# Loading a matrix of 113 rows in two transfers, 112 rows and one

## The chip, the cores and the metric

The kernel runs on one core of a Trainium2 chip. The core has five engines with an instruction queue each: TensorE (PE, matmuls, with a row of its own for weight loads, PEld), VectorE (DVE), ScalarE (ACT), GpSimd (POOL) and SyncE (SP, which only issues transfers here). Sixteen DMA engines move the data between the device memory and the core; SyncE, GpSimd and ScalarE give them their work. The metric is the time of one execution on the device in microseconds, the median of several.

## The reference, cut to what matters

A block of two parts with a residual each: a state-space convolution (S4) over 2048 positions and 576 channels with 128 complex states per channel, and a gated MLP that mixes positions. Both are modulated by six vectors made from a condition vector `c`.

```python
x = A_u
mod = (_silu(c) @ w_mod).reshape(c.shape[0], 6, 1, -1)
sa, ca, ga, sb, cb, gb = (mod[:, i] for i in range(6))
h = _layernorm(x) * (1 + ca) + sa
x = x + ga * ssm(h, A_re, A_im, B_re, B_im, C_re, C_im, log_dt, Dskip)
h = _layernorm(x) * (1 + cb) + sb
x = x + gb * mlp(h, w_in, w_sp, b_sp, w_out)

# ssm: K[d, l] = Re sum_n C[d, n] * exp(dt[d] * A[d, n] * l) * dt[d] * B[d, n], dt = exp(log_dt)
#      y = the causal convolution of h with K (by FFTs of length 4096) + h * Dskip
```

## The kernel before, in words

The function `ssm` makes the convolution, the class `Mlp` the rest. The change lies in the first lines of `ssm` that issue work.

**What the start makes.** Three strands run beside each other in the first 90 us. The *poles*: for each state, the logarithm of its decay, its phase and so on are computed on VectorE and ScalarE from seven inputs (`poles`), split into three bfloat16 parts, written to the device memory (`pa_d`, `pb_d`) and read back in another layout as the tiles `lb`, `lc` and `la` (`poles_load`). `p0` is this for the first 144 channels (tile `et` as staging), `p1` for the other 432 in one go (tiles `t_n_...`, steps `q`). The *modulation*: for each k, `mod_load` brings a part of `w_mod` (two transfers of 96 rows; tile `wm` or `k`), `mod_mm` multiplies it with silu(c), `mod_ev` copies the partial sums out (`mpart`), `mod_on` sums them over the partitions by a matmul with a matrix of ones, and `mod_fin` stores the row (`gar`, `cga`, `sga`). The matrix of ones is the last of six 128x128 matrices in the tile `small`. The *norm of the input*: `ln_load` brings x (tile `ln_x`), `ln_stat` makes mean and variance, `ln_row` and `ln_mm` go on with it.

**The selection matrix.** `sel` is a tile of 113 partitions and 2368 bfloat16 columns, read from `c_sel`. Matmuls with `lb`, `lc` or `la` as weights and columns of `sel` as the moving operand (`e_mm`, `ec_mm`, `phase`, `t_unit`) spread the poles over times. They read rows 0 to 47 and 64 to 111, or 0 to 111; those of `phase` with x = 0 read rows 0 to 48 and 64 to 112. Row 112 holds constants for these alone.

**What sets the order.** In the opening every engine runs its instructions in the order of the program (`tied`, class `Pinned`); SyncE, too. SyncE's transfers are, in this order: seven of the poles, `cT` (c), two of `wm` (k = 2), `sel`, two of `k` (k = 1), `small`, two of `lb`, two each of `lc` and `la`, seven of `t_n_...`, `dsk`. GpSimd's are the writes of the poles, `ln_x`, `k` (k = 0), `r1t`, `cs`, `msk` and the second `ln_x`. After that the string `OPENING` names one step after the other; it begins with

```python
"mo 2;mm 1;ml 3;mg 2;me 1;eA 0;w 0 0;mo 1;EA 0;w 0 1;eB 0;..."
"EA 2;mm 0;EB 2;mf 1;q 0;r 0;a 0;me 0;q 1;mo 0;mf 0;q 2;c 0;..."
```

where `mo` is `mod_on`, `mm` is `mod_mm`, `eA` is `e_mm`, `a` and `c` are `phase`, and `q 0` starts `p1` with the activation `t_dt`. From about 207 us to about 445 us a loop over ticks makes the rest of the convolution, and there the order on an engine is planned by the program's scheduler; behind it stretches are written out again.

Of the kernel before, what the change touches and what calls it, by code (L numbers as in the profile page):

```python
# [121 lines left out]
def body(tc, I, out):  # L122
    nc = tc.nc
    V, A, G, T, S = nc.vector, nc.scalar, nc.gpsimd, nc.tensor, nc.sync
    with ExitStack() as ctx:
        dram = ctx.enter_context(tc.tile_pool(name="dram", bufs=1, space=DRAM))
        keep = ctx.enter_context(tc.tile_pool(name="keep", bufs=1))

        x1_d = dram.tile([16, 128, D], F32, name="x1_d")

        consts_s = keep.tile([128, 4], F32, name="consts_s")
        V.memset(consts_s[:, 0:1], MAGIC)
        V.memset(consts_s[:, 1:2], math.pi / 2)
        V.memset(consts_s[:, 2:3], 1.0)
        V.memset(consts_s[:, 3:4], 0.0)
        mod_d = dram.tile([3, D], F32, name="mod_d")
        acc = keep.tile([128, 96], F32, name="acc")
        m = Mlp(tc, ctx, I, x1_d, dram, mod_d, acc, out)
        ssm(tc, I, x1_d, consts_s, dram, mod_d, m)
        m.phase_a()  # L140
        m.phase_b()
# [47 lines left out]
def ssm(tc, I, x1_d, consts_s, dram, mod_d, mlp):  # L189
    nc = tc.nc  # L190
    V, A, G, T, S = nc.vector, nc.scalar, nc.gpsimd, nc.tensor, nc.sync
# [3 lines left out]
    with ExitStack() as ctx:  # L195
# [22 lines left out]
        sel = tb.tile([113, 2368], BF, name="sel", bufs=1)  # L218
# [109 lines left out]
        def poles_tile(c, Q):  # L328
            for n, p in (("lb", 112), ("lc", 113), ("la", 113)):
                lt[n, c] = tb.tile([p, 9, 128], BF, name=n)  # L330
                Q.memset(lt[n, c][32:64], 0.0 if n == "lb" else 1.0)
                if n != "lb":
                    Q.memset(lt[n, c][96:113], 1.0)
# [35 lines left out]
        def mod_load(k, Q):  # L369

            if k < 2:
                t = kp.tile([128, 32, 128], F32, name="k1").rearrange("p a b -> p (a b)")
                wmt[k] = [t[:96, 6 * HC * hh:6 * HC * hh + 6 * HC].rearrange("p (k n) -> p k n", k=6) for hh in range(2)]
            else:
                wmt[k] = [ep.tile([96, 6, HC], F32, name="wm") for hh in range(2)]
            for hh in range(2):
                Q.dma_start(wmt[k][hh], I["w_mod"][:, k, hh])
# [434 lines left out]
        V, A, G, T, S = mlp.tied.vector, mlp.tied.scalar, mlp.tied.gpsimd, mlp.tied.tensor, mlp.tied.sync  # L812
        p0 = poles(0, 1, G, tb.tile([128, 1536], F32, name="et", bufs=5))
        S.dma_start(cT, I["c"])
        mod_load(2, S)
        S.dma_start(sel, I["c_sel"])
        mod_load(1, S)
        S.dma_start(small, I["c_small"][:, 128:].rearrange("p (i c) -> p i c", i=6))
        poles_tile(0, G)
        for _ in range(4):  # L820
            next(p0)
# [38 lines left out]
        V, A, G, T, S = nc.vector, nc.scalar, nc.gpsimd, nc.tensor, nc.sync  # L860
# [40 lines left out]
        V, A, G, T, S = mlp.nc.vector, mlp.nc.scalar, mlp.nc.gpsimd, mlp.nc.tensor, mlp.nc.sync  # L901
# [1427 lines left out]
```

## Time and profile before

| | us |
|---|---|
| median of 3 runs | 1800.42 (1796.09 to 1802.07) |
| the profiled execution | 1799.91 |
| its span | 1798.0 |
| TensorE busy | 1673.5 (93%) |
| VectorE busy | 1244.5 (69%) |
| ScalarE busy | 819.0 (46%) |

The span runs from the first to the last instruction of the profiled execution; the time of that execution has 1.9 us more around it. Engines work beside each other, so their busy times don't add up to the span. The timeline gives start, duration, engine, line, operation, and in brackets how long the engine was idle before it and what released it; nearly every line reads L154, because a helper records the pinned instructions there, so tiles tell them apart. For a transfer the timeline shows its issue on the queue's engine, and the DMA issues give the time to its landing.

### The profile page before, as it was taken

The numbers are of one execution on the slowest core, as the hardware profiler recorded it, in microseconds if no ns is written. First come the engines' busy times: TensorE is split into PE (matmuls) and PEld (weight loads), VectorE is DVE, ScalarE is ACT, GpSimd is POOL, SyncE is SP. The second block draws the span as 40 slices with busy tenths as digits, with TensorE's granted clock in tenths as the row PEclk, the third lists the DMA queues.
The fourth block names the chain that finished last, engine by engine and source line by source line (L and its number), as shares of the span: only waits on it lengthen the run. The fifth ranks groups of instructions, "written<-read, shape, count | busy, mean of one in ns | idle before, by whom it ended". The sixth has DMA issues, their size and how long they took to land.

```text
span 1798.0 us, 36706 instructions
## 1 busy us (share of the span) xinstructions
PE 1673.5 (93%) x15374; PEld 1247.2 (69%) x15374; DVE 1244.5 (69%) x2242; ACT 819.0 (46%) x1095; POOL 252.6 (14%) x397
## 2 busy tenths in 40 slices
PE   0498899998799989999999999999999999999999
PEld 0154555565455544777877888887888888888887
DVE  4576589975898998788899677689344468344432
ACT  1477799864377666444534343334222124122110
POOL 2023234233122212000000000000111100111100
PEclk7669999999899999999999999999999999999999
DMA  7355946579778778777674887773666573556531
GB/s 206 82 159 172 262 128 176 167 200 291 233 230 279 253 235 268 255 264 254 241 234 140 282 289 264 240 264 124 229 237 221 202 234 107 188 201 207 202 110 41
DMA packets 181468, 376.28 MB, mean 209 GB/s; under 512 B 38325, under 2 KB 101429, under 8 KB 180534
## 3 DMA queue, kind: packets, MB, share of 16 engines
q1 hardware_dynamic: 137766, 171.43, 31.6%
q0 software_dynamic: 37632, 175.83, 29.6%
q10 hardware_dynamic: 5904, 26.67, 3.6%
q8 instruction: 121, 1.98, 0.5%
q14 instruction: 45, 0.37, 0.1%
HBM read 263.12 MB, written 101.31 MB: 203 GB/s over the span
## 4 chain that ended last, share of the span: by engine, by line
PE 42%; DVE 18%; issue 9%; DMA 7%; ACT 3%; POOL 1%; ACTq 0%; SPq 0%; DVEq 0%; POOLq 0%
PE ps L154 40%; DMA zset<-set_d 4%; DVE zset L154 4%; DVE gt L154 2%; DVE bsz L154 2%; DMA raw<-z_d 1%; ACT z L154 1%; DVE n L154 1%; DVE rq L154 1%; DVE wsp L154 1%; DVE raw L154 1%; DVE wout L154 1%; DVE wso L154 1%; DVE z L154 1%; DMA uu<-v_d 1%
## 5 line engine op out<-in xcount | busy, mean ns | idle before, releaser
L154 PEld LDWEIGHTS <-zset 128*128 128x128 f16 x7182 | 702.7, 98 | 95.5 <-DVE zset L154 7.5
L154 PE MATMUL ps<-wsp,zset 128*128 128x256 f16 x6048 | 669.4, 273 | 9.0 <-DVE zset L154 5.8
L154 PE MATMUL pz<-wz,nt 128*128 128x512 f16 (+1 forms) x1120 | 222.3, 358 | 11.2 <-DVE nt L154 4.3
L154 ACT ACTIVATE z<-gt 128x1024 f16<-128x1024 f32 x56 | 59.0, 1054 | 292.6 <-DVE gt L154 292.6
L154 PEld LDWEIGHTS <-nt 128*128 128x128 f16 x1120 | 108.9, 98 | 118.3 <-DVE nt L154 5.8
L2037 POOL DMA_DIRECT2D zset<-set_d x96 | 50.8, 530 | 872.4 <-PE ps L154 632.1
L154 DVE SCALAR_TENSOR_TENSOR gt<-ps,sc,bsp 128x512 f32<-128x512 f32 x36 | 27.0, 750 | 207.2 <-PE ps L154 205.5
L154 PE MATMUL ps<-wout,z 128*128 128x288 f16 x1344 | 170.0, 286 | 0.0
L154 PEld LDWEIGHTS <-z 128*128 128x128 f16 x1344 | 131.5, 98 | 33.0
L154 DVE TENSOR_TENSOR raw<-raw 128x512 f32<-128x512 f32 (+2 forms) x228 | 119.2, 528 | 14.7 <-DMA raw<-z_d 10.4
L154 PE MATMUL ps<-n2o,zset 128*128 128x256 f16 x1134 | 128.2, 273 | 0.0
L154 DVE SCALAR_TENSOR_TENSOR gt<-ps,sc,gt 128x512 f32<-128x512 f32 (+1 forms) x180 | 122.2, 696 | 7.6
L154 ACT ACTIVATE zset<-raw 128x1792 f16<-128x1792 f32 x48 | 81.0, 1690 | 55.3 <-PE ps L154 18.7
L154 DVE TENSOR_TENSOR zset<-raw,zset 128x1792 f16<-128x1792 f32 x48 | 96.9, 2019 | 13.1 <-ACT zset L154 13.1
L154 DVE TENSOR_TENSOR z<-ps,z 128x512 f32<-128x512 f32 (+1 forms) x126 | 72.0, 599 | 37.2 <-ACT z L154 26.7
L154 ACT ACTIVATE wsp<-raw,sc 128x1792 f16<-128x1792 f32 x25 | 44.6, 1785 | 43.1 <-DVE raw L154 35.4
L154 ACT ACTIVATE z<-z,sc 128x1024 f32<-128x1024 f32 x21 | 24.1, 1148 | 76.0 <-DVE z L154 72.3
L154 ACT ACTIVATE z<-pz,sc 128x512 f32<-128x512 f32 (+1 forms) x96 | 51.6, 583 | 12.7 <-PE pz L154 6.1
L154 ACT ACTIVATE z<-z,nm,r 128x1152 f32<-128x1152 f32 x24 | 31.5, 1342 | 56.7 <-DVE nm L154 31.4
L154 PE MATMUL ps<-n2q,wf 128*128 128x512 f16 x252 | 55.7, 379 | 0.0
L154 PE MATMUL ps<-wout,z1b 128*128 128x288 f16 x384 | 52.4, 286 | 0.0
L154 DVE SCALAR_TENSOR_TENSOR wsp<-raw,sc,wsp 128x1792 f16<-128x1792 f32 x25 | 52.0, 2078 | 0.0
(353 smaller groups left out, 2441.7 us busy)
## 6 DMA issues: line engine op xcount, KB each, us to landing
zset<-set_d POOLq DMA_DIRECT2D x96, 896.0 KB, 4.9
raw<-z_d SPq DMA_DIRECT2D x48, 512.0 KB, 5.6
set_d<-zset ACTq DMA_DIRECT2D x24, 896.0 KB, 6.6
z_d<-z POOLq DMA_DIRECT2D x32, 576.0 KB, 9.2
zset<-wa_d POOLq DMA_DIRECT2D x18, 896.0 KB, 4.9
raw<-in_w_spT SPq DMA_DIRECT2D x25, 512.0 KB, 5.0
set_d<-zset SPq DMA_DIRECT2D x12, 896.0 KB, 4.6
u_d<-st1o POOLq DMA_DIRECT2D x16, 576.0 KB, 4.1
```

The costliest lines, as they stand in the source:

```text
L154: return self.tc.keep_in_program_order(f(*a, **k))
L2037: self.nc.gpsimd.dma_start(o, self.set_d[f, j - 1] if j else self.wa_d[f])
```

## The change

The load of `sel` is split. The first 112 rows go where the whole load was, the last row goes behind `small`. Nothing else differs: the same bytes go to the same tile on the same queue.

```diff
         S.dma_start(cT, I["c"])
         mod_load(2, S)
-        S.dma_start(sel, I["c_sel"])
+        S.dma_start(sel[:112], I["c_sel"][:112])
         mod_load(1, S)
         S.dma_start(small, I["c_small"][:, 128:].rearrange("p (i c) -> p i c", i=6))
+        S.dma_start(sel[112:], I["c_sel"][112:])
         poles_tile(0, G)
```

## The prediction

> **What bounds the kernel now.** I read the page's head and its 40 slices first, then the waits of TensorE over the first 70 us, because a load issued in the first microseconds can only matter there. Columns of the waits: waiting engine and tile, what ended the wait, us in total, times, longest.
>
> ```profile
> span 1798.0 us, 36706 instructions
> PE   0498899998799989999999999999999999999999
> ...
> PE ps L154 <- DMA small<-in_c_small: 39.4, 1, 39.4
> ```
>
> The span is 1798.0 us and the execution took 1799.9 us. In the first slice of 45 us TensorE is hardly busy; later it is busy nearly always. One wait of 39.4 us, for the small matrices, makes that hole. The timeline (start, us, engine, line, operation) shows what is in the queue around it:
>
> ```profile
> 5.44 0.33 SPq L154 DMA_DIRECT2D sel<-in_c_sel  x1
> 5.82 12.12 SPq L154 DMA_DIRECT2D k<-in_w_mod  x2
> 17.27 0.75 POOL L154 DMA_DIRECT2D pb_d<-pt  x1
> 17.98 3.40 SPq L154 DMA_DIRECT2D small<-in_c_small  x1
> 22.32 0.78 POOL L154 DMA_DIRECT2D pa_d<-pt  x1 [3.74 <-DVE pt L154]
> 25.79 4.34 SPq L154 DMA_DIRECT2D lb<-pb_d  x2
> 50.08 2.25 SPq L154 DMA_DIRECT2D la<-pa_d  x2
> 53.58 0.42 SPq L154 DMA_DIRECT2D t_n_log_dt<-in_A_log_dt  x1
> 54.43 0.38 SPq L154 DMA_DIRECT2D t_n_A_im<-in_A_A_im  x1
> 54.55 2.26 PE L154 MATMUL ps<-mpart,small 128*128 128x288 f32 x4 [39.40 <-DMA small<-in_c_small]
> 56.74 3.32 PE L154 MATMUL ps<-k,ec 96*32 96x288 f32 x24
> 59.99 0.39 PE L154 MATMUL ps<-sel,lb 48*128 48x512 bf16 x2
> 66.42 0.58 ACT L154 ACTIVATE t_dt<-t_n_log_dt 128x432 f32<-128x432 f32 x1
> 71.68 0.60 DVE L154 TENSOR_TENSOR t_q<-t_n_C_im,t_n_B_im 128x432 f32<-128x432 f32 x1
> ```
>
> The sel load takes 0.33 us to issue, and right behind it two loads hold SyncE for 12.12 us. What the transfers move meanwhile is in the windows (stretch, length, busy times and counts of PE, PEld, DVE, ACT, POOL, granted clock, DMA share, GB/s):
>
> ```profile
> 6.00:8.00 2.00, 0.00 (x0) 0.00 (x0) 1.91 (x8) 0.00 (x1) 0.11 (x1) 1.00 0.88 276
> 8.00:10.00 2.00, 0.00 (x0) 0.00 (x0) 1.92 (x7) 0.61 (x1) 0.00 (x0) 1.00 0.97 252
> 10.00:12.00 2.00, 0.70 (x8) 0.39 (x10) 1.83 (x8) 1.95 (x5) 0.00 (x0) 1.00 0.36 96
> 12.00:14.00 2.00, 2.00 (x18) 0.75 (x12) 0.47 (x3) 1.83 (x5) 0.00 (x0) 1.00 0.06 26
> 44.00:46.00 2.00, 0.00 (x0) 0.00 (x0) 0.00 (x0) 0.00 (x0) 0.00 (x0) 0.50 0.07 28
> ```
>
> From 12 to 14 us, and again from 44 to 46, the share is 0.06 to 0.07 of 16 DMA engines: one engine works, at 26 to 28 GB/s, and fifteen stand still. Which transfer it is, the DMA issues (KB each, median us to landing), the tile view of the k loads (ns of one, shortest, median, longest; first and last start) and SyncE's own waits say:
>
> ```profile
> sel<-in_c_sel SPq DMA_DIRECT2D x1, 522.6 KB
> k<-in_w_mod SPq DMA_DIRECT2D x2, 648.0 KB, 37.6
> small<-in_c_small SPq DMA_DIRECT2D x1, 384.0 KB, 36.4
> pa_d<-pt POOLq DMA_DIRECT2D x3, 108.0 KB, 8.0
> t_n_log_dt<-in_A_log_dt SPq DMA_DIRECT2D x1, 216.0 KB, 6.2
> ...
> L154 SPq DMA_DIRECT2D k<-in_w_mod x2: 1999/6040/10081, 5.8 to 15.9; - x2
> ...
> SPq L154 <- DMA sel<-in_c_sel: 14.1, 1, 14.1
> SPq L154 <- DMA pb_d<-pt: 4.3, 1, 4.3
> ```
>
> 522.6 KB are 0.535 MB; at 26 GB/s one engine needs 20.6 us for them, and longer while the transfers of POOL's queue share that engine from 15 to 44 us. SyncE waited 14.1 us for sel before la, so sel landed just before 50.08, 44.6 us after its issue. The second k load (issued at 15.9, 37.6 to its landing) landed at 53.5 and small at 17.98 + 36.4 = 54.4: both hold a small share on the same engine behind sel. TensorE's next matmul is at 54.55. la needs nothing of sel; it waits because it is the 19th transfer of SyncE and sel the 11th. In the same way the 21st (t_n_log_dt, 53.58) starts when the 13th (k) lands and the 22nd (t_n_A_im, 54.43) when the 14th (small) does: a transfer starts only when the one eight before it is done. So sel's landing holds the start of TensorE directly and the pole loads through SyncE.
>
> **The change part by part.** 113 rows become 112 and one. Nothing is computed otherwise; SyncE issues one transfer more.
>
> *Spread of the 112 rows.* The trace has no load of 112 rows. The nearest rows are the 96-row loads of w_mod, which run in the windows 6 to 10 us at a share of 0.88 to 0.97 and 252 to 276 GB/s, and the 113-row load at 0.06. 96 and 112 are multiples of 16, 113 is not; I take the 96-row end, 0.535 MB / 264 GB/s = 2.0 us, and keep the other end as a rival. The Trainium skill (DMA: Bandwidth & Descriptors, section on why a DMA increments its semaphore by 16) says that a transfer uses the largest number of engines up to 16 that divides the slowest dimension of both sides; by it 113 rows get one engine and 112 get 16, and no run so far shows 112.
>
> *small.* The w_mod loads end near 10.6 us (0.36 in the window 10:12 is 0.32 of it full and the rest at 0.06). From there sel, two k (2 x 648.0 KB = 1.327 MB) and small (0.393 MB) are 2.26 MB; at 264 GB/s, 8.5 us. Four writes of the poles (two each of pa_d and pb_d, 108.0 KB, 0.44 MB) come in between, 1.7 us. small lands at 20.8 instead of 54.4. TensorE then runs the 2.26 us on small and the 3.32 us on k, 5.4 us from first to second end (54.55 to 59.99), and is done at 26.2.
>
> *lb.* The next matmul reads lb, which is loaded when the write of 17.27 has landed.
>
> ```profile
> DMA to landing us min/median/max: 2.3/2.9/8.4
> ...
> L154 SPq DMA_DIRECT2D la<-pa_d x2: 696/698/699, 50.1 to 51.6; - x2
> ...
> DMA to landing us min/median/max: 2.4/3.3/9.8
> ```
>
> These are the landings of the pb_d writes, the issues of la (ns of one), and the landings of the pa_d writes. In the trace SyncE went on at 25.79; with less in the way I take 24 (bounds 20 and 25.8). Two issues of 0.7 us and a landing between the fastest pole write (2.3) and t_n_log_dt (6.2), say 3.6, make 29 for lb (bounds: 26.2, when TensorE is free, and 33). The matmul at 59.99 moves to 29. The activation t_dt stood 6.4 us behind it: 35.4.
>
> *Pole loads.* lc and la read the write of 22.32; landing by 29 (24.7 to 32.1). Four issues at 0.7 us: t_n_log_dt is issued at about 32, the last of the seven, B_im, 2.5 us later. The landings are set by all that has to be moved:
>
> ```profile
> DMA packets 3919, 9.14 MB, mean 185 GB/s; under 512 B 382, under 2 KB 2394, under 8 KB 3662
> ...
> DMA packets 998, 4.71 MB, mean 294 GB/s; under 512 B 159, under 2 KB 159, under 8 KB 801
> ```
>
> The first line is 10.6 to 60 us, the second 24 to 40. The 9.14 MB at 294 GB/s take 31.1 us, at 264 take 34.6: the whole opening's traffic ends between 41.7 and 45.2, I take 43, instead of at 60. B_im is read 5.3 us after t_dt (66.42 to 71.68), so t_dt can't be earlier than about 37.9 if B_im is last. That is later than 35.4, so it decides: 66.4 - 37.9 = 28.5 us, rounded to 28. What is late next is therefore transfer bandwidth, no longer one engine.
>
> *Bounds.* Early: lb at 26.2 and the pole loads ahead of POOL's last load give t_dt at 32.6, a gain of 33.8. Late: the poles issued at 35, and their 1.55 MB at half of 264 GB/s, 11.7 us, give B_im at 46.7 and t_dt at 41.4, a gain of 25.
>
> *One issue more.* 4.7 KB at 25 GB/s are 0.2 us, and an issue is 0.33 to 0.43 us. It lies in SyncE's wait of 4.3 us for pb_d; without that cover it costs 0.4 us ahead of lb and all behind it. The matmuls on rows 64 to 112 may wait for it, but it goes right behind small, which TensorE needs first. In the count of eight, la now looks back on k instead of sel, landed by then in either case.
>
> *After t_dt* the order of every engine is written out, and nothing in it has a fixed time; I let the 28 us through to the end. **Sum:** 1799.9 - 28 = 1771.9, **1772 us**. The profiled time is within 0.5 us of the median of 1800.4, so no correction is made.
>
> **The rivals.**
>
> *A, most of the way, less through the clock.* TensorE's work would come in short pieces with gaps, and the granted clock might stay at half.
>
> ```profile
> 60.00:75.00 15.00, 8.52 (x67) 4.16 (x66) 9.50 (x18) 8.24 (x12) 0.00 (x0) 0.93 0.47 120
> 105.00:120.00 15.00, 12.62 (x198) 7.38 (x197) 10.66 (x18) 13.75 (x26) 4.31 (x6) 0.59 0.36 119
> 120.00:135.00 15.00, 14.43 (x208) 8.45 (x210) 11.35 (x31) 12.40 (x23) 2.45 (x4) 0.77 0.61 177
> 150.00:165.00 15.00, 11.27 (x140) 6.17 (x140) 10.27 (x20) 9.47 (x12) 1.76 (x3) 0.89 0.62 178
> ...
> 207.00:445.00 238.00, 223.38 (x2903) 136.11 (x2897) 188.74 (x246) 180.29 (x241) 85.08 (x138) 1.00 0.72 196
> ```
>
> At 0.50 instead of 0.93 the 8.52 us would grow by 7.3; 27.05 us at 0.50 instead of a mean of 0.68 by 9.7. In the worst case 17 us go: 1772 + 17 = 1789, or 1775 + 17 = 1792 from the late bound. Against it: the hole goes from 39 us to about 6, and DVE and ACT carry part of that stretch. Equally, an earlier warm clock could bring some us more. Chance 0.09 for 1787 to 1792.
>
> *B, it does not do what it says.* If 112 rows still went through one engine, sel would land 0.4 us earlier and one issue would be added: 1800, no change. Against: no full transfer of 96 or 128 rows shows 0.06. The Trainium skill (DMA: Bandwidth & Descriptors, Rules for kernel authors) advises against two transfers for disjoint parts of the partitions, since both spread over the same engines anyway; by that rule the split gives nothing. The trace disagrees for this load, at 0.06. Chance 0.06.
>
> *C, slower.* From 207 to 445 us the order on each engine is not written out but planned from estimated times, and a transfer more may change the plan. TensorE is busy 223.4 of 238 us there, 94%. If a new order left it the 75% of the stretch 150 to 165, the stretch would last 297 us, 59 longer: 1772 + 59 = 1831. It decides from a loss of 28 us, a share below 84%. For it: nothing pins that stretch. Against: the plan's inputs change by a transfer of 4.7 KB. Chance 0.05, 1806 to 1831.
>
> **How the numbers follow.** Forecast 0.80; A 0.09, B 0.06, C 0.05. The forecast's bounds, 25 to 33.8 us, give 1766 to 1775; with two thirds of A's price, 12 us, on one side, and 6 us of an earlier warm clock on the other, 1760 to 1787. That holds 0.80 and leaves the rivals out. Faster by over 0.3% (5.4 us, about what a measurement of this kernel can tell from no change) is forecast and A, 0.89; within it B, 0.06; slower C, 0.05.
>
> **What would show it.** Right: no stretch at a share of 0.06 between 10 and 50 us; k issued in under 1 us each; small landing in about 14 us, TensorE's wait for it ending near 21; the matmul on sel and lb near 29, t_dt near 37; the last slice reached some 28 us earlier with the same busy times. Wrong: the share at 0.06 again after sel's issue (B); TensorE held past 30 us by another landing; t_dt near 37 but the end not moved (A, by the clock, or C, by the stretch from 207 us on).

## The result and the profile after

The kernel with the two transfers takes 1772.05 us in the median of four executions (1769.84 to 1774.06), the kernel before in the same comparison 1800.7 (1796.09 to 1802.07): a ratio of 0.9845 with an interval of 0.9824 to 0.9866. The forecast was 1772.0. The profiled execution is the slowest of the four, 1774.06 us with a span of 1772.2, so its trace shows 25.8 us of the gain, and the sums below are made against that.

The head of the page after, and the waits of TensorE and of SyncE over the start (what waits, for what, us in total, times, longest):

```profile
span 1772.2 us, 36706 instructions
PE 1679.9 (95%) x15374; PEld 1248.7 (70%) x15374; DVE 1244.5 (70%) x2242; ACT 820.3 (46%) x1095; POOL 252.6 (14%) x397
PE   4688999997899999999999999999999999999999
...
PE ps L154 <- DMA lb<-pb_d: 5.6, 1, 5.6
PE ps L154 <- DMA small<-in_c_small: 4.7, 1, 4.7
...
SPq L154 <- DMA pb_d<-pt: 14.4, 1, 14.4
```

The busy times are what they were to within 7 us, the hole at the start is smaller. The wait for `small` fell from 39.4 to 4.7 us, and a new one, for `lb`, is TensorE's longest wait for a transfer in its place. SyncE no longer waits for `sel`; it is early now, and waits for the pole write that it needs. The same strand as before in the timeline after:

```profile
5.44 0.42 SPq L154 DMA_DIRECT2D sel<-in_c_sel  x1
5.91 1.12 SPq L154 DMA_DIRECT2D k<-in_w_mod  x2
7.08 0.46 SPq L154 DMA_DIRECT2D small<-in_c_small  x1
7.58 0.33 SPq L154 DMA_DIRECT2D sel<-in_c_sel  x1
20.02 2.26 PE L154 MATMUL ps<-mpart,small 128*128 128x288 f32 x4 [4.67 <-DMA small<-in_c_small]
22.47 1.65 SPq L154 DMA_DIRECT2D lb<-pb_d  x2
25.91 1.69 SPq L154 DMA_DIRECT2D la<-pa_d  x2
27.65 0.45 SPq L154 DMA_DIRECT2D t_n_log_dt<-in_A_log_dt  x1
33.44 0.61 PE L154 MATMUL ps<-sel,lb 48*128 48x512 bf16 x1 [5.62 <-DMA lb<-pb_d]
39.57 0.62 ACT L154 ACTIVATE et<-pk 128x512 f32<-128x512 f32 x1
43.08 0.53 SPq L154 DMA_DIRECT2D t_n_B_im<-in_A_B_im  x1
43.91 0.56 ACT L154 ACTIVATE t_dt<-t_n_log_dt 128x432 f32<-128x432 f32 x1 [3.73 <-DMA t_n_log_dt<-in_A_log_dt]
```

The two k loads take 1.12 us to issue in place of 12.12, and `small` is issued at 7.08 in place of 17.98. The windows after, where one engine had worked alone before (the last three numbers are the granted clock, the DMA share and GB/s):

```profile
12.00:14.00 2.00, 2.00 (x17) 0.75 (x12) 0.47 (x2) 1.83 (x5) 0.00 (x0) 1.00 1.05 291
14.00:16.00 2.00, 1.35 (x6) 0.18 (x2) 1.62 (x8) 1.17 (x5) 1.16 (x2) 1.00 1.03 259
```

All sixteen engines are at work, at some ten times the rate. Where the 25.8 us came from can be read off by the lead of one trace over the other at instructions that occur once in both:

| Instruction | before, us | after, us | lead |
|---|---|---|---|
| copy of the first modulation row (gar) | 56.84 | 22.32 | 34.5 |
| t_dt | 66.42 | 43.91 | 22.5 |
| copy of a later row (gar, with consts_s) | 163.26 | 140.62 | 22.6 |
| activation sc<-ones at the end of the convolution | 450.75 | 427.25 | 23.5 |
| end of the span | 1798.0 | 1772.2 | 25.8 |

So 34.5 us were there early, 12 were given back by t_dt, and 3.3 came in the 1700 us behind it. The order of the instructions on TensorE, VectorE, ScalarE and GpSimd is the same in both kernels.

### The profile page after: what moved, and what is told of

It is laid out like the page before. It is cut to its first block, busy times and chain, and to the rows that moved or that the text cites. A ratio compares the mean times of both kernels' runs of the same rounds, so it can differ in the third digit from the quotient of the medians.

```text
span 1772.2 us, 36706 instructions
## 1 busy us (share of the span) xinstructions
PE 1679.9 (95%) x15374; PEld 1248.7 (70%) x15374; DVE 1244.5 (70%) x2242; ACT 820.3 (46%) x1095; POOL 252.6 (14%) x397
## 4 chain that ended last, share of the span: by engine, by line
PE 55%; DVE 12%; issue 7%; DMA 5%; ACT 2%; POOL 1%; SPq 0%; ACTq 0%; DVEq 0%; POOLq 0%
PE ps L154 49%; PE pz L154 4%; DMA zset<-set_d 3%; DVE bsz L154 1%; DVE zset L154 1%; DVE wsp L154 1%; DVE n L154 1%; DVE gt L154 1%; DVE rq L154 1%; DMA uu<-v_d 1%; ACT z L154 1%; DVE nt L154 1%; DVE wso L154 1%; PE pk L722 0%; DVE rx L154 0%
## 5 line engine op out<-in xcount | busy, mean ns | idle before, releaser
L154 DVE TENSOR_TENSOR raw<-raw 128x512 f32<-128x512 f32 (+2 forms) x228 | 119.0, 528 | 12.4 <-DMA raw<-z_d 8.1
L154 DVE TENSOR_TENSOR zset<-raw,zset 128x1792 f16<-128x1792 f32 x48 | 96.9, 2019 | 15.4 <-ACT zset L154 15.4
L154 ACT ACTIVATE wsp<-raw,sc 128x1792 f16<-128x1792 f32 x25 | 44.6, 1785 | 43.1 <-DVE raw L154 35.2
```

The lines of the kernel that those rows point to most:

```text
L154: return self.tc.keep_in_program_order(f(*a, **k))
```

## The experiments

**e0, the kernel before once more.** No edit. It is to show how far one execution differs from the next.

> The kernel before, unchanged, for a second profile. In the two profiles at hand the lead of the changed kernel is 34.5 us at the copy of the modulation row (gar), 22.4 us from t_dt (66.42 against 43.91) to 142 us, 23.0 at 300 us and 25.8 at the end. Theory V, the 3.4 us that come after 142 us are what one execution differs from the next: the span between 142 us and the end then differs between the two profiles of before by 1 to 5 us. Rival N, they belong to the change: that span agrees within 0.5 us.

1798.86 us, span 1797.1, beside 1798.0 of the first profile: the ends agree within 0.9 us, but not the way there. At the later row it is 0.4 us behind, at sc<-ones 3.8 us behind (454.58 against 450.75), and by the end 0.9 us ahead. The window in which it falls behind, first in the trace of before, then in that of e0:

```profile
165.00:180.00 15.00, 14.53 (x271) 8.11 (x265) 5.77 (x10) 12.87 (x20) 2.30 (x3) 1.00 0.33 115
```

```profile
165.00:180.00 15.00, 14.89 (x236) 8.03 (x234) 5.68 (x10) 9.83 (x15) 1.71 (x3) 0.67 0.23 80
```

TensorE is as busy, but the clock is granted at 0.67 in place of 1.00, and 35 matmuls fewer get done. The same kernel thus loses 4 us and wins nearly 5 back along the way. In its own terms theory V holds narrowly: from the later row to the end the two profiles differ by 1.3 us, within its 1 to 5, but less than the 3.3 us to be explained. The other profiles show more. From t_dt to the end of the span the two of the kernel before took 1731.6 and 1730.6 us, the three of the changed kernel (this one, e4 and e8) 1728.3, 1724.4 and 1726.4, and that of e5, which differs from it only in the place of one row, 1732.1. So 3.3 us lie within what executions differ by; that a little of it belongs to the change isn't excluded.

**e1, one transfer of 113 rows, behind small.** It separates the place of the load from its shape.

```diff
-        S.dma_start(sel, I["c_sel"])
         mod_load(1, S)
         S.dma_start(small, ...)
+        S.dma_start(sel, I["c_sel"])
```

> All 113 rows in one transfer again, but issued behind small. Theory E (one DMA engine moves all 113 rows, and what is queued behind it waits): small lands near 18 us, but the share of 0.06 is back at some time between 20 and 50 us, sel lands between 36 and 48, the first matmul on sel and lb comes then, t_dt 6 us later; 8 to 22 us slower than the two transfers, 1780 to 1794. Rival P (only the place ahead of k and small was wrong): as fast as the two transfers, 1769 to 1775.

1792.1 us in the median (1788.12 to 1802.41, ten executions) against 1796.53 of the kernel before; ratio 0.998 (0.9961 to 0.9999). TensorE's part of the timeline, SyncE's wait and two windows:

```profile
18.37 2.26 PE L154 MATMUL ps<-mpart,small 128*128 128x288 f32 x4 [3.20 <-DMA small<-in_c_small]
20.56 2.67 PE L154 MATMUL ps<-k,ec 96*32 96x288 f32 x24
55.73 1.30 PE L154 MATMUL ps<-sel,lb 48*128 48x512 bf16 x2 [32.51 <-DMA lb<-pb_d]
...
SPq L154 <- DMA sel<-in_c_sel: 5.7, 1, 5.7
...
44.00:46.00 2.00, 0.00 (x0) 0.00 (x0) 0.00 (x0) 0.00 (x0) 0.00 (x0) 0.50 0.07 28
52.00:54.00 2.00, 0.00 (x0) 0.00 (x0) 0.00 (x0) 0.00 (x0) 0.00 (x0) 0.50 0.06 26
```

`small` is there even earlier than with two transfers (18.4 against 20.0), and it brings next to nothing: the wait has moved to `lb`, issued behind `sel`. t_dt is at 63.4. Rival P falls. The lone engine is back, and SyncE's wait for `sel` ends at 54.9, where the 22nd transfer (t_n_A_im) starts, eight behind `sel` as 14th. `sel` landed later than I had expected, 36 to 48. I had left out that GpSimd's transfers share that engine: by the packet records of the trace 44 of the rows were moved from 16 to 36 us, when GpSimd's queue was busy, and 21 in the 4 us from 48 to 52.

**e2, 111 rows and 2.** Does any number that isn't a multiple of 16 go through one engine?

```diff
-        S.dma_start(sel[:112], I["c_sel"][:112])
+        S.dma_start(sel[:111], I["c_sel"][:111])
...
-        S.dma_start(sel[112:], I["c_sel"][112:])
+        S.dma_start(sel[111:], I["c_sel"][111:])
```

> Rows 0 to 110 in one transfer and the last two behind small. Theory E with the divisor rule (111 is 3 x 37, so three engines): 175 KB an engine, 6.7 us at 26 GB/s, small lands at 21 to 26 instead of 19.9, the end at 1772 to 1780. Rival M (a number of rows that is no multiple of 16 goes to one engine): the share of 0.06 again, as before the change, 1798 to 1802. Rival P (place alone): 1772.

1779.12 us (1775.73 to 1782.0) against 1796.53; ratio 0.9908 (0.9872 to 0.9944). The waits of TensorE and the issue of `small`:

```profile
PE ps L154 <- DMA small<-in_c_small: 20.8, 1, 20.8
...
small<-in_c_small SPq DMA_DIRECT2D x1, 384.0 KB, 29.3
```

`small` was issued at 6.76 and landed 29.3 us later, at 36.1; between 54.4 with 113 rows and 20 with 112. So M falls and P again: it isn't one engine, and it isn't all. No window shows three engines alone, but the packet records of the traces bear the three out. Each row of `sel` is one packet of 4736 bytes, and of these never more than two are in flight at once with 113 rows, most often four with 111, and most often 17 with 112: one more than 1, 3 and 16 engines, as a packet often starts shortly before the one ahead of it on its engine ends. The landing of `small` is 10 us later than my sum for three, which again had nothing for GpSimd's transfers; that they are the reason isn't shown. t_dt is at 49.4, 17.0 us ahead of before, and the median 17.4.

**e3, 113 rows in one transfer, issued by GpSimd.**

```diff
-        S.dma_start(sel, I["c_sel"])
+        G.dma_start(sel, I["c_sel"])
```

> All 113 rows in one transfer, issued by GpSimd in place of SyncE. If GpSimd's queue spreads 113 rows over its engines (theory E allows it, since the rule for an uneven number is that of SyncE's queue), no stretch at 0.06, small lands near 20, 1768 to 1778. If one engine takes them there too: the pole writes behind them on GpSimd's queue wait, and k and small share one engine with them, 1790 to 1802.

1775.84 us (1770.84 to 1778.19) against 1796.53; ratio 0.9881 (0.9849 to 0.9913). The issue and a window:

```profile
sel<-in_c_sel POOLq DMA_DIRECT2D x1, 522.6 KB, 5.8
...
12.00:14.00 2.00, 1.15 (x12) 0.58 (x16) 1.41 (x7) 1.95 (x5) 0.00 (x0) 1.00 0.98 249
```

GpSimd has nothing to do at first and issues the load at 1.29, where SyncE came to it at 5.44. The same 522.6 KB, unsplit, land 5.8 us after the issue, and no engine is left alone. t_dt is at 43.4, as with two transfers (43.9). What costs the time is thus neither the 113 rows nor their bytes but how SyncE's queue spreads them. The Trainium skill (DMA: Bandwidth & Descriptors, section on why a DMA increments its semaphore by 16) says that some copies issued by GpSimd get 16 engines where the divisor rule would give fewer; its examples are 100 and 127 partitions. The trace agrees, with 5.8 us against 44.6.

**e4 and e5, two transfers again, and the last row at once.** e4 has no edit. e5 puts the last row right behind the 112:

```diff
         S.dma_start(sel[:112], I["c_sel"][:112])
+        S.dma_start(sel[112:], I["c_sel"][112:])
         mod_load(1, S)
```

> The changed kernel, unchanged, on the chip of the next three, as their yardstick and for a second profile. In the three runs so far the median moved by about as much as t_dt did (e1: 4.4 us against 3.0; e2: 17.4 against 17.0; e3: 20.7 against 23.0, against the kernel before on the same chip). Theory T (the lead at t_dt is what reaches the end): t_dt at 43 to 45 and the median 20 to 25 us ahead of the kernel before. Rival N (the change brings some 3 to 6 us more, later on): 26 to 31 us ahead again.

> The last row right behind the 112 rows, ahead of k and small. Theory E (only the 112 rows' spread counts; the row is 4.7 KB, 0.2 us of one engine): t_dt within 1 us of the two transfers, the median within 3 us. Rival O (the row must be out of the way of k and small): small lands over 1 us later, t_dt as well.

e4: 1774.2 us (1770.66 to 1775.79) against 1797.4, ratio 0.9872 (0.9846 to 0.9897), t_dt at 44.5. e5: 1775.82 (1770.88 to 1778.36), ratio 0.9874 (0.9843 to 0.9906), t_dt at 44.5. In e5 TensorE had `small` at 22.2 in place of 20.4 in e4, 1.8 us later, as rival O has it; but t_dt didn't move, as theory E has it, because the wait for t_n_log_dt ends later, at 44.5 in both. The place of the last row is worth nothing that shows at the end. The 23.2 us of e4 speak for theory T.

**e6 and e7, where the 12 us were given back.** Between the copy of the first row and t_dt the changed kernel loses a third of its lead. t_dt waits for t_n_log_dt, issued at 27.65 and landed 16.2 us later. That wait is the last 3.7 us of the 12; ScalarE was free for t_dt only at 40.2, because TensorE had waited 5.6 us for `lb`. The load of t_n_log_dt, and the queues of the changed kernel from 24 to 40 us (packets, MB, share of the 16 engines):

```profile
t_n_log_dt<-in_A_log_dt SPq DMA_DIRECT2D x1, 216.0 KB, 16.2
...
q0 software_dynamic: 646, 3.32, 76.4%
q1 hardware_dynamic: 997, 0.92, 21.2%
```

q0 is GpSimd's, q1 SyncE's. Packets of 5.1 KB stand against packets of 0.92 KB (MB by packets). e6 takes the second `ln_x` load off GpSimd's queue; e7 issues the pole loads ahead of lc and la as well:

```diff
-        ln_load(1, G)
         S.dma_start(dsk, I["dsk"])
+        ln_load(1, S)
```

```diff
+        p1 = poles(1, 4, G)
         poles_load(0, S, ("lc", "la"))
-        p1 = poles(1, 4, G)
```

> The changed kernel with the second ln_x load (1.18 MB, first read some 16 us after t_dt) taken from GpSimd's queue and issued by SyncE behind dsk. Theory S (after the change the pole loads are late because GpSimd's queue, with packets of 5.1 KB against 0.9 KB, takes three quarters of the engines from 24 to 40 us): t_n_log_dt lands 16.2 us after its issue now and would land 4 us earlier; t_dt at 40 to 41 in place of 43.9 (ScalarE is free for it at 40.2), the end 3 to 5 us earlier. Rival I (SyncE's issues, or lb, set t_dt): t_dt stays at 43 to 44.

> As e6, and the seven t_n loads issued ahead of lc and la. Theory S: t_n_log_dt is issued at about 24.3 in place of 27.7 and lands before ScalarE is free at 40.2, A_im too; then lc and la, behind 1.55 MB more, come late for the first phase matmuls (read at 42.8 in the changed kernel). t_dt at 40 to 41, the end as e6 within 2 us. Rival I: t_dt as in the changed kernel.

e6: 1768.91 us (1766.88 to 1775.74), ratio 0.9852 (0.9821 to 0.9882). e7: 1772.44 (1771.24 to 1773.7), ratio 0.9865 (0.9841 to 0.9888). The same queues and window in e6, and ScalarE there:

```profile
q0 software_dynamic: 540, 2.23, 53.4%
q1 hardware_dynamic: 1884, 1.53, 37.0%
...
t_n_log_dt<-in_A_log_dt SPq DMA_DIRECT2D x1, 216.0 KB, 12.4
...
40.73 0.62 ACT L154 ACTIVATE et<-pk 128x512 f32<-128x512 f32 x1
41.21 0.59 ACT L154 ACTIVATE t_dt<-t_n_log_dt 128x432 f32<-128x432 f32 x1
```

With 1.09 MB less on GpSimd's queue SyncE's moves 1.53 MB in place of 0.92, t_n_log_dt lands 12.4 us after its issue, and the wait in front of t_dt is gone: it follows ScalarE's last copy without a pause. Theory S holds for the landing; whether the size of GpSimd's packets or only their amount was in the way isn't shown, as e6 takes away an amount. Then `lb`'s landing is what sets t_dt (TensorE waits for it until 34.6 in e6), and so e7 gains nothing on e6: t_dt 41.1 against 41.2.

**e8 and e9, the changed kernel and e6 in five rounds.**

> The changed kernel in five rounds, as the yardstick of the next. Theory T (the lead at t_dt, 22 to 23 us, reaches the end): 20 to 25 us ahead of the kernel before. Rival N (some 3 to 6 us more, later on): 26 to 31 ahead.

> The kernel of e6 in five rounds. In its profile t_dt stood at 41.2 against 44.5 in the changed kernel on the same chip. Theory T: 2 to 5 us ahead of the changed kernel in the median. Rival V (what one execution differs from the next hides it): within 1 us of it.

e8: 1777.35 us (1769.66 to 1779.23) against 1798.42, ratio 0.9868 (0.9845 to 0.9891). e9: 1772.98 (1769.15 to 1777.51), ratio 0.9849 (0.9824 to 0.9874). The medians of e6 and e9 lie 5.3 and 4.4 us below those of the changed kernel beside them, but the ranges overlap, and in e9's profile t_dt is at 43.5 against 43.7 in e8: `lb` came late in that execution (TensorE got it at 37.0), so there t_dt is where rival I had it. That t_n_log_dt lands sooner is shown, 12.6 us after its issue in e9 against 16.5 in e8; that the kernel is faster for it isn't settled. Against the kernel before e6 is clearly faster, as the changed kernel is.

## Why the prediction was right, and where it was not

*What bounds the start.* Right, and shown. One engine carried the 113 rows, and everything queued behind them on it waited. e1 keeps the shape and mends the order, and wins 4.4 us of some 23; e3 keeps the shape and changes the queue, and wins 20.7.

*The spread of the 112 rows, and small.* Right. `small` was put at 20.8 and came at 20.0; TensorE was to be done with k at 26.2 and was at 26.3; there `small` was 0.8 us early and the matmuls on k 0.7 us slower than in the trace of before (4.05 us against 3.32). The issue more cost nothing that shows.

*lb.* Too early. 29 was said, with bounds of 26.2 and 33; the first matmul on it started at 27.23, the second had to wait until 33.44 for the other half. SyncE went on at 22.47, sooner than the 24 of the sum, so it is the landing, put at 3.6 us, that was too short. By this path alone t_dt would have come at 40.2, when ScalarE was free, and not at 35.4.

*The pole loads.* This is the step that was mis-sized: t_dt was put at 37.9 with bounds of 32.6 and 41.4, and came at 43.91. (43 less 5.3 is 37.7, not 37.9; the slip is small beside the miss.) The sum took the whole traffic, 9.14 MB at 264 GB/s, had no term for how the two queues share the engines, and let B_im, the last of the seven loads, decide. The rate was right: 265 GB/s were moved from 24 to 40 us in the changed kernel. But SyncE's queue got only 21.2% of the engines, so already the first of the seven, t_n_log_dt, came late and decided, though it was issued at 27.65 and not at 32. The seven issues were put at 2.5 us from first to last and took 15.4 (27.65 to 43.08). The gain at t_dt was 22.5 us in place of 28.5, outside the 25 to 33.8 that I gave for it.

*After t_dt.* "I let the 28 us through to the end" was right in kind: what was there at t_dt reached the end. In the profiled pair 3.3 us were added on the way, within what executions differ by. That the total came out at 1772 to a tenth is luck: a gain that was 6 us too large at t_dt met a comparison on the favourable side, 28.6 us there by the medians, against 23.2 in e4 and 21.1 in e8. All three medians of the changed kernel, 1772.05, 1774.2 and 1777.35, lie within 1760 to 1787, and the intervals of the three ratios overlap.

*The rivals.* A, the clock: TensorE did run slowly through this stretch (605 ns for a matmul of 386, shown below), but t_dt waited for a transfer 3.7 us beyond the work in front of it, so nothing was lost to the clock there. B fell by the windows at 12 to 16 us. The rule of the Trainium skill that is cited beside it (DMA: Bandwidth & Descriptors, Rules for kernel authors), that two transfers for parts of the partitions bring nothing, presumes that either way all the engines are used; here the measurement decides against it. C fell: the order on those four engines didn't change.

## What to carry to other kernels

Look for a stretch in which the DMA share stands at a small fixed fraction: 0.06 is one engine of sixteen, and the transfer in question holds back not only its own reader but all that is queued behind it on that engine. Of the three counts tried on SyncE's queue, 113 (a prime) was worst, 111 (3 x 37) lay between and 112 (7 x 16) was best. A load with an unlucky count can be split so that most of it has a good one, or, as here, issued by GpSimd; moving it behind the others only moved the wait. Once the engines are all at work, the next bound is how the queues share them: loads on one queue can hold back those of another.

## What the runs showed of the hardware that was not expected

**The granted clock in the rows can be wrong.** In the changed kernel every window from 20 to 50 us has a granted clock of 1.00. The matmuls on `sel` and `lb` (ns of one: shortest, median, longest), first in the kernel before from 60 us on, then in the changed kernel:

```profile
L154 PE MATMUL ps<-sel,lb x6: 372/386/387, 60.0 to 63.9; 48*128 48x512 bf16 x6
```

```profile
L154 PE MATMUL ps<-sel,lb x6: 582/605/606, 27.2 to 37.7; 48*128 48x512 bf16 x6
```

The same six matmuls take 605 ns in place of 386, which is how long they take in the kernel before where the rows grant 0.50 to 0.59 (606 at 103.7 to 107.4 us). In two other traces of such an opening the rows do follow the matmuls: in e6 they grant 0.50 from 36 to 38 us, with the same 0.61 us for one, and 1.00 from 38.9 to 40 us, with 0.39; in e8 0.50 from 31 to 35 us, with 0.61, and 1.00 from 35.6 to 36.4, with 0.39. So TensorE was slow in the changed kernel's first trace, too, and the row doesn't say so. The Trainium skill (TensorE: Matmul & The Clock Gate, Seeing it yourself, the caveats on the trace of the clock gate) warns that these events have been seen to be unreliable; the trace agrees. The duration of a known matmul is the better gauge.

**Issuing a transfer can take long.** Behind the 113 rows the two k loads held SyncE for 12.12 us before, and 1.12 after; in e1 the lb loads behind them took 12.47 us to issue. A transfer on one engine thus costs its queue's issues, too, not only its own landing. It isn't the lone engine alone: in the changed kernel, with all engines at work, one load, t_n_A_re, took 6.53 us to issue. That SyncE's queue is full at such times is likely, but not shown.
